# Linear attention into a tanh-shrink MLP: two loads swapped, the work of batch 1 and the phi of batch 2 spread over later slots, two matmuls moved ahead of a spread

## The chip, the cores and the metric

The kernel runs on one core of one Trainium2 chip. The metric is the device time of one execution in microseconds (us). Executions of one kernel agree within some 0.4%; the clock granted to TensorE was 0.997 to 1.0. Times inside an execution are us from the start of its span, as the profile gives them.

## The reference, cut to what matters

```python
q, k, v: (8, 8, 576, 64) float32; w_in: (512, 2048); w_out: (2048, 512)
phi(x) = where(x > 0, x, exp(x) - 1) + 1
kv  = einsum('bhsd,bhse->bhde', phi(k), v);   z = sum(phi(k), axis=2)
num = einsum('bhsd,bhde->bhse', phi(q), kv)
den = einsum('bhsd,bhd->bhs', phi(q), z)[..., None] + 1e-6
x   = (num / den), laid out as (4608 tokens, 512)
h   = x @ w_in;   out = (h - tanh(h)) @ w_out
```

## The kernel before

TensorE does nine chunks of 512 tokens. A chunk has a first matmul in 16 column blocks of 4 matmuls (h = x w_in), then a second one in 16 slots of 4 (g w_out). The attention of the next batch is slipped in between: `s1[fi]` holds what follows column block fi, `s2[s]` what follows slot s. Each engine runs its own list in program order. `xT` is x transposed, its four head pairs being p = 0 to 3.

From chunk 1 on the first matmul goes round six PSUM banks; a pair of blocks is freed when VectorE has written `gT` from it:

```python
dense = Banks([0, 1, 2, 3, 4, 5])       # block 10 of chunk 1 comes to bank 4 again, block 4's
attn = Banks([6, 7])                    # kv, denominators and numerators of the next batch
def l1act2(fi, h, gT):                  # after each odd block
    th = mpool.tile([128, 2, 512], F32, name="th")
    nc.scalar.activation(th, h, AF.Tanh)
    nc.vector.tensor_sub(gT[:, fi:fi + 2, :], h, th)
```

phi is an exp on ScalarE and two operations on VectorE, called the rest below:

```python
e = exp(x)                  # ScalarE
r = max(x, 0) + 1           # VectorE
y = min(e, r)               # VectorE
```

For batch 1 and most of batch 0 a spread (a group of small matmuls with `sel`) copies each head's reciprocal denominators to the partitions where they are needed. From batch 2 on the reciprocal denominators go through memory: four small writes to `ds`, then two broadcasting reads into `rdb`, all on SyncE's queue; the numerators are scaled with `rdb`.

```python
def a_spread(b):
    ...
    for t in range(4):
        nc.sync.dma_start(out=ds[:, t, :], in_=rden_t[b][32 * t:32 * t + H, :])
    ...
    for hh in range(2):
        nc.sync.dma_start(out=rdb[64 * hh:...], in_=ds[4 * hh:...].partition_broadcast(64))

def a_num(b, p):            # two banks, so numerator 3 waits until numerator 1 is scaled
    ps = num_mm(b, p, attn)
    nc.vector.tensor_mul(xT[:, p, ...], ps, rdb[:, p, ...])
```

The loads of batch c + 2 (k, q, v) are issued at the start of chunk c by GpSimd, behind a gate that reads the last column of the transposed q of batch c + 1, so they wait for that transposing DMA, which is on SyncE's queue as well, in order with the output stores:

```python
s1[0].append(lambda: (gate(qT_t[n1]), load_k(n2), load_q(n2), load_v(n2)))
```

## Time and profile before

| | us |
|---|---|
| time, median of 3 runs at first | 293.31 (293.09 to 293.58) |
| span of the profiled run | 291.8 |
| TensorE busy | 285.5 |
| VectorE, ScalarE busy | 175.1, 139.7 |
| second matmul of chunk 0 starts | 31.07 |
| first and second matmul of chunk 1 start | 50.24, 65.93 |
| third numerator of chunk 1; chunk 2 starts | 79.31; 80.72 |

TensorE's ends are modelled, so idle time is not read from the busy sum but from starts: a start, plus the number of matmuls times 0.216, against the next group's start. The prediction shows the lines.

### The profile page before, as it was taken

The numbers are of one execution on the slowest core, as the hardware profiler recorded it, in microseconds if no ns is written. First come the engines' busy times: TensorE is split into PE (matmuls) and PEld (weight loads), VectorE is DVE, ScalarE is ACT, GpSimd is POOL, SyncE is SP. The second block draws the span as 40 slices with busy tenths as digits, with TensorE's granted clock in tenths as the row PEclk, the third lists the DMA queues.
The fourth block names the chain that finished last, engine by engine and source line by source line (L and its number), as shares of the span: only waits on it lengthen the run. The fifth ranks groups of instructions, "written<-read, shape, count | busy, mean of one in ns | idle before, by whom it ended". The sixth has DMA issues, their size and how long they took to land.

```text
span 291.8 us, 4505 instructions
## 1 busy us (share of the span) xinstructions
PE 285.5 (98%) x1803; PEld 134.5 (46%) x1803; DVE 175.1 (60%) x266; ACT 139.7 (48%) x168; POOL 33.7 (12%) x56
## 2 busy tenths in 40 slices
PE   8999999999999999999999999999999999999994
PEld 3544464454454444444454444444544444444443
DVE  4759958987468674776478637865581457106600
ACT  4938548846354733465345534751551155126411
POOL 8674030110030003000300030000000000000000
PEclk9999999999999999999999999999999999999999
DMA  7999999997999768965895579666117310130032
GB/s 105 193 202 212 208 206 215 194 183 149 249 158 161 175 128 137 197 146 121 136 223 123 123 139 197 146 138 139 30 38 165 73 36 0 43 83 19 0 74 72
DMA packets 39093, 38.94 MB, mean 133 GB/s; under 512 B 16352, under 2 KB 33824, under 8 KB 38304
## 3 DMA queue, kind: packets, MB, share of 16 engines
q0 software_dynamic: 17568, 18.35, 39.0%
q1 hardware_dynamic: 21344, 20.17, 30.9%
q8 instruction: 14, 0.23, 0.3%
q10 hardware_dynamic: 160, 0.13, 0.1%
q14 instruction: 7, 0.06, 0.1%
HBM read 43.91 MB, written 9.55 MB: 183 GB/s over the span
## 4 chain that ended last, share of the span: by engine, by line
PE 85%; DMA 11%; POOL 2%; issue 1%; DVE 0%; POOLq 0%
PE ps_all L387 39%; PE ps_all L366 38%; DMA v<-in_v_dram 6%; DMA w_in_sb<-in_moe_w_in_dram 3%; PE ps_all L199 2%; DMA kraw<-in_k_dram 2%; PE ps_all L317 2%; PE ps_all L618 1%; PE ps_all L276 1%; POOL v L419 1%; PE ps_all L177 1%; POOL qraw L90 0%; PE ps_all L320 0%; POOL qraw L93 0%; POOL w_out_sb L115 0%
## 5 line engine op out<-in xcount | busy, mean ns | idle before, releaser
L366 PE MATMUL ps_all<-xT,w_in_sb 128*128 128x512 bf16 x574 | 127.6, 379 | 0.0
L387 PE MATMUL ps_all<-w_out_sb,gT 128*128 128x512 bf16 x560 | 127.5, 379 | 0.0
L373 DVE TENSOR_TENSOR gT<-ps_all,th 128x1024 bf16<-128x1024 f32 x64 | 77.9, 1218 | 59.2 <-ACT th L372 59.2
L372 ACT ACTIVATE th<-ps_all 128x1024 f32<-128x1024 f32 x64 | 65.6, 1025 | 57.1 <-PE ps_all L366 46.5
L366 PEld LDWEIGHTS <-w_in_sb 128*128 128x128 bf16 x574 | 55.0, 98 | 66.1 <-issue 0.3
L387 PEld LDWEIGHTS <-gT 128*128 128x128 bf16 x560 | 54.2, 98 | 64.2
L396 ACT COPY osb<-ps_all 128x512 f32<-128x512 f32 (+1 forms) x36 | 20.9, 583 | 71.8 <-PE ps_all L387 52.6
L328 DVE TENSOR_TENSOR xT<-ps_all,rdb 128x512 bf16<-128x512 f32 x24 | 16.5, 691 | 13.7 <-PE ps_all L317 11.2
L134 ACT ACTIVATE e<-qraw 128x1152 bf16<-128x1152 bf16 x16 | 18.5, 1160 | 8.2 <-DMA qraw<-in_q_dram 8.2
L134 ACT ACTIVATE e<-kraw 128x1152 bf16<-128x1152 bf16 x15 | 17.5, 1164 | 0.3 <-DMA kraw<-in_k_dram 0.3
L136 DVE TENSOR_TENSOR qp<-e,r 128x1152 bf16<-128x1152 bf16 x16 | 12.1, 758 | 8.0 <-ACT e L134 7.2
L136 DVE TENSOR_TENSOR kp<-e,r 128x1152 bf16<-128x1152 bf16 x15 | 11.4, 759 | 7.9 <-ACT e L134 6.9
L383 POOL COPY g<-qT 1x1 bf16<-1x1 bf16 x5 | 0.9, 178 | 119.2 <-DMA qT<-qp 119.2
L378 DVE TENSOR_TENSOR gT<-ps_all,th 128x512 bf16<-128x512 f32 x16 | 10.3, 686 | 2.4 <-ACT th L377 1.7
L377 ACT ACTIVATE th<-ps_all 128x512 f32<-128x512 f32 x16 | 9.2, 598 | 4.4 <-PE ps_all L366 3.2
L447 PE MATMUL ps_all<-zero 128*128 128x512 bf16 x29 | 9.2, 480 | 1.2 <-DVE zero L405 1.2
L317 PE MATMUL ps_all<-qT,kz 128*128 128x512 bf16 x28 | 10.1, 379 | 0.0
L135 DVE TENSOR_SCALAR r<-qraw 128x1152 bf16<-128x1152 bf16 x16 | 7.3, 454 | 2.1 <-DMA qraw<-in_q_dram 2.1
L199 PEld LDWEIGHTS <-kp 64*128 64x128 bf16 x216 | 6.4, 94 | 2.5 <-issue 2.1
L285 DVE RECIPROCAL rden<-den 128x144 f32<-128x144 f32 x7 | 7.4, 1053 | 0.2
L199 PE MATMUL ps_all<-vp,kp 64*128 64x136 bf16 x216 | 7.4, 220 | 0.0
L394 DVE COPY osb<-ps_all 128x128 f32<-128x128 f32 x1 | 0.3, 292 | 11.6 <-PE ps_all L618 11.6
(85 smaller groups left out, 123.6 us busy)
## 6 DMA issues: line engine op xcount, KB each, us to landing
out_dram<-osb SPq DMA_DIRECT2D x70, 128.0 KB
rdb<-ds SPq DMA_DIRECT2D x12, 576.0 KB
kraw<-in_k_dram POOLq DMA_DIRECT2D x7, 576.0 KB, 7.1
qraw<-in_q_dram POOLq DMA_DIRECT2D x7, 576.0 KB, 9.1
v<-in_v_dram POOLq DMA_DIRECT2D x7, 576.0 KB, 11.6
w_in_sb<-in_moe_w_in_dram POOLq DMA_DIRECT2D x6, 256.0 KB, 8.7
w_out_sb<-in_moe_w_out_dram POOLq DMA_DIRECT2D x3, 512.0 KB, 14.7
qraw<-in_q_dram POOLq DMA_DIRECT2D x2, 288.0 KB, 4.4
```

What stands on the lines that cost most here:

```text
L134: return (lambda: nc.scalar.activation(e, x, AF.Exp), lambda: nc.vector.tensor_scalar(r, x, 0.0, 1.0, ALU.max, ALU.add), lambda: nc.vector ...
L136: lambda: nc.vector.tensor_tensor(y, e, r, ALU.min))
L199: nc.tensor.matmul(ps[hg][:, i, :], kp[r, i, j].rearrange("p h d -> p (h d)"), vp[r, i, j, :], start=(j == 0), stop=(j == J - 1))
L317: nc.tensor.matmul(ps, kz[:, p // 2, p % 2, 0:128], qT[:, p % 2, 0:8, p // 2, :], start=True, stop=True)
L328: nc.vector.tensor_mul(xT[:, p, S * b:S * b + 512].rearrange("p (j t c) -> p j t c", j=8, t=4), ps.rearrange("p j (t c) -> p j t c", t=4), ...
L366: nc.tensor.matmul(h, w_in_sb[:, 2 * (p % 2) + p // 2, fi * 128:(fi + 1) * 128], xT[:, p, c * 512:(c + 1) * 512], start=(n == 0), stop=(n ...
L372: nc.scalar.activation(th, h, AF.Tanh)
L373: nc.vector.tensor_sub(gT[:, fi:fi + 2, :], h, th)
L377: nc.scalar.activation(th, h, AF.Tanh)
L378: nc.vector.tensor_sub(gT[:, fi, :], h, th)
L387: nc.tensor.matmul(o, gT[:, fi, i * 128:(i + 1) * 128], w_out_sb[:, fi, :], start=(fi == 0), stop=(fi == NF - 1))
L396: nc.scalar.copy(osb[:, f0:f1], o[:, f0:f1])
```

## The change

Its intent, as far as the code shows it: kv of batch 1 no longer waits for v (half a quarter of w_out, wanted first, is loaded first, and kv goes from slot 7 to slot 9); the rests of phi make room for xT on VectorE; and the opening does two matmuls ahead of a spread. With these come two moves: kv and the denominators of batch 2 (`a_den`, `a_spread`) come two column blocks later in chunk 1, and the transposing DMA of its q (`a_qT_dma(2)`) goes from slot 13 to slot 15 of chunk 0.

```diff
-    load_v(1)
     for n in range(2):
+        if n == 1:
+            load_v(1)
         nc.gpsimd.dma_start(out=w_out_sb[:, 8 + 2 * n:10 + 2 * n, :], ...)
 ...
-            s2[7].append(lambda: (a_qT_pe(1, 0, side), a_kv(1, side), a_qT_pe(1, 1, side)))
-            s2[8].append(lambda: b0_scale_rest(side))
-            s2[9].append(lambda: (a_den(1, side), num1(), a_split(1)))
-            s2[11].append(lambda: spread1(0))
+            s2[7].append(lambda: a_qT_pe(1, 0, side))
+            s2[8].append(lambda: a_qT_pe(1, 1, side))
+            s2[9].append(lambda: a_kv(1, side))
+            s2[10].append(lambda: (b0_scale_rest(side), a_den(1, side), num1(), a_split(1)))
+            s2[12].append(lambda: spread1(0))
 ...
-            s2[11].append(lambda: (exp2(qs, q_t, qp_t, "qp", 0), rest2(qs[0])))
+            s2[11].append(lambda: exp2(qs, q_t, qp_t, "qp", 0))
             s2[12].append(lambda: exp2(qs, q_t, qp_t, "qp", 1))
-            s2[13].append(lambda: (spread1(1), exp2(ks, k_t, kp_t, "kp", 0), rest2(qs[1]), a_qT_dma(2)))
-            s2[14].append(lambda: rest2(ks[0]))
+            s2[14].append(lambda: (spread1(1), exp2(ks, k_t, kp_t, "kp", 0), rest2(qs[0])))
+            s2[15].append(lambda: (rest2(qs[1]), a_qT_dma(2)))
 ...
-            s1[8 if c == 1 else 5].append(lambda: a_kv_cols(n1, attn))
-            s1[10 if c == 1 else 8].append(lambda: (a_den(n1, attn), a_spread(n1)))
+            s1[10 if c == 1 else 5].append(lambda: a_kv_cols(n1, attn))
+            s1[12 if c == 1 else 8].append(lambda: (a_den(n1, attn), a_spread(n1)))
 ...
-            s1[1].append(lambda: a_kphi(2, 1))
-            s1[3].append(lambda: (a_vp(2, 0), a_vp(2, 1)))
+            s1[1].append(lambda: (exp2(ks, k_t, kp_t, "kp", 1), rest2(ks[0])))
+            s1[3].append(lambda: rest2(ks[1]))
+            s1[5].append(lambda: (a_vp(2, 0), a_vp(2, 1)))
 ...
-            order = [((0, 0), (0, 1)), ((2, 0), (2, 1), (0, 2), (0, 3), (2, 2), (2, 3)),
+            order = [((0, 0), (0, 1)), ((2, 0), (2, 1)), ((0, 2), (0, 3), (2, 2), (2, 3)),
 ...
-                if n == 1:
+                if n == 2:
                     open2()          # the second spread
 ...
-            if c == 2 and fi == 1:   # blocks 0 and 1: pairs 0, 1 of both, then pairs 2, 3
+            if c in (1, 2) and fi == 1:
 ...
-            elif c != 2 or fi > 1:
+            elif c not in (1, 2) or fi > 1:
```

## The prediction

> **What bounds the kernel now.** First the page. TensorE is busy for 98% of the span at full clock, so I look for the few tenths in which it waits.
>
> ```profile
> PE 285.5 (98%) x1803; PEld 134.5 (46%) x1803; DVE 175.1 (60%) x266; ACT 139.7 (48%) x168; POOL 33.7 (12%) x56
> ...
> PEclk9999999999999999999999999999999999999999
> ```
>
> Then TensorE's own timeline (start, length, engine, line, instructions). Sixty-two 512-column matmuls begin at 17.68 and the next group at 31.07: 13.39/62 = 0.216 us each. With that cadence I find every hole. The first transposes of batch 1 take nine times 0.058, to 38.50; kv starts at 38.87. A step from full-size matmuls to a smaller tile costs 0.10 wherever it occurs (80.72 + 24 x 0.216 = 85.90, kv at 86.00), so 0.27 of that hole is the wait for v. The second spread, 17.02, waits about 0.4. At 46.20 there is 0.1 over the step.
>
> ```profile
> 17.02 0.73 PE L240 MATMUL ps_all<-rden,sel 32*128 32x128 f32 x16 [0.22 <-DVE xT L244]
> 17.68 13.55 PE L366 MATMUL ps_all<-xT,w_in_sb 128*128 128x512 bf16 x62
> 31.07 7.07 PE L387 MATMUL ps_all<-w_out_sb,gT 128*128 128x512 bf16 x32
> 37.98 0.67 PE L164 MATMUL ps_all<-ident,qp 128*128 128x128 bf16 x9
> 38.87 1.66 PE L177 MATMUL ps_all<-v,kp 64*128 64x192 bf16 x36 [0.22 <-DMA v<-in_v_dram]
> ...
> 50.24 8.07 PE L366 MATMUL ps_all<-xT,w_in_sb 128*128 128x512 bf16 x36
> ```
>
> Chunk 1's first matmuls, from 50.24, need 36 x 0.216 = 7.77 and take 7.91 up to the 0.10 step before kv at 58.24: 0.14 of waiting. So all that can be gained is about 0.4 + 0.27 + 0.1 + 0.14 = 0.9 us.
>
> Third, the timelines of VectorE and ScalarE around the start of chunk 1, because three parts of the change move work there. The reader should see how full they are.
>
> ```profile
> 51.77 0.45 DVE L135 TENSOR_SCALAR r<-kraw 128x1152 bf16<-128x1152 bf16 x1
> 52.33 0.76 DVE L136 TENSOR_TENSOR kp<-e,r 128x1152 bf16<-128x1152 bf16 x1
> 53.50 1.23 DVE L373 TENSOR_TENSOR gT<-ps_all,th 128x1024 bf16<-128x1024 f32 x1 [0.41 <-ACT th L372]
> 54.64 0.45 DVE L135 TENSOR_SCALAR r<-kraw 128x1152 bf16<-128x1152 bf16 x1
> 55.19 0.76 DVE L136 TENSOR_TENSOR kp<-e,r 128x1152 bf16<-128x1152 bf16 x1
> 55.87 1.22 DVE L373 TENSOR_TENSOR gT<-ps_all,th 128x1024 bf16<-128x1024 f32 x1
> 57.00 0.82 DVE L189 COPY vp<-v 128x1152 bf16<-128x1152 bf16 x2
> 57.74 2.35 DVE L373 TENSOR_TENSOR gT<-ps_all,th 128x1024 bf16<-128x1024 f32 x2
> ```
>
> Back to back, a gT pair costs VectorE 1.13, a phi rest (r and kp) 1.23, the vp pair 0.74. ScalarE is tied to the landing of q of batch 2: exp at 47.34, four evacuations and two more exps, tanh at 52.41.
>
> Fourth, the end of chunk 1. The scaling there waits for rdb, the broadcast reciprocal, which lands at about 77.8.
>
> ```profile
> 77.87 1.48 DVE L328 TENSOR_TENSOR xT<-ps_all,rdb 128x512 bf16<-128x512 f32 x2 [2.39 <-DMA rdb<-ds]
> ```
>
> Its chain: den at 61.24, rden ready 64.06, the small ds writes issued at 64.09 but done only at 69.4, rdb issued at 69.44, landing 8.4 later. The DMA share falls from 1.19 to 0.69 at 68 to 69 us: the small writes finish just after the loads of batch 3.
>
> **What the Trainium skill says.** "PSUM — Partial Sum Buffer", section "PSUM bank collisions raise a hardware error", tells one to guard PSUM by bank and quadrant, not by address. The trace agrees: the second spread writes other columns than VectorE is reading, yet starts at 17.02, just after the reader ended at 16.97. "TensorE: Matmul & The Clock Gate", section "Architectural detail: the array is 16× 32×32, not 1× 128×128", says that ScalarE and VectorE are strict FIFO; here the rests and gT pairs do run in program order, so a late one delays all behind it. "DMA: Bandwidth & Descriptors", section "Issuing engines are not separate DMA queues", says that transfers of all issuers share 16 engines and interleave; the ds writes that take 5.3 us under the loads and 2.3 (92.72 to 95.00) at their end agree.
>
> **The change part by part.**
>
> *w_out before v.* Landings before, from issue plus time to landing: q 35.9, v 38.8, first half quarter 40.05, second 41.35, last quarter 43.85. The queue moves 256 KB in about 1.25 us, so the half quarter now lands near 37.2 and v near 40.05; everything behind is where it was, q of batch 2 at 47.2 included. Slot 8 needs w_out near 38.6 and kv in slot 9 needs v near 41: neither waits. Gain 0.27.
>
> *Opening.* The two matmuls need the same xT as the spread waited for, so they start at 17.02 too. The spread then pays its 0.10 step in the open, and xT of the third pair arrives 0.05 too late. Loss about 0.15.
>
> *Slots 7 to 15.* The same work, walked with the measured pieces from 38.13 (37.98 and the opening's 0.15): transposes 0.52, slot 8 0.86, transposes 0.52, slot 9 0.86, step and kv 0.10 + 1.59, slot 10 0.86, the rest of batch 0 0.11, step and den 0.10 + 0.36, which is 44.01. VectorE's kz is ready 1.0 after kv (43.6), in time for den at 43.65. Numerators 0.11 + 0.86, slots 11 and 12 1.73: 46.71. The split's result followed den's first matmul by 3.2 before (42.91 to 46.14), so the first spread starts at 46.94 with 0.13 of wait, about what it had. Spread 0.23, two slots 1.73, step and spread 0.33, slot 15 0.86: chunk 1 begins at 50.1 instead of 50.24. On ScalarE exp of k moves behind the third evacuation, which removes the 0.14 wait for bank 2; the fourth ends at 52.50 (47.34 + three exps of 1.07 + four copies of 0.46, with small rounding), still ahead of bank 3's use at 52.72. The chain from q's landing has the same members, so tanh of the first pair is again at 52.4 and its gT at 53.48. The interleaving of matmuls covers the later xT (pair 3 ready 50.83, wanted 51.2).
>
> *Phi of k in chunk 1.* This is where I expect the loss. Both rests of k now lie between the gT pairs: gT01 53.48, rest 54.62, gT23 55.85, rest 56.98, gT45 58.21, done 59.43. Before, 0.74 of vp lay between gT23 and gT45; now 1.23. TensorE meanwhile comes sooner to bank 4, which gT45 frees for column block 10, because kv and its step (1.27) moved from behind block 8 to behind block 10: 50.1 + 0.04 + 10 x 0.864 = 58.8 plus 0.08 of wait on gT23 = 58.85. It waits until 59.48: 0.63. Then six blocks (5.18), kv (1.27), den (0.46): the second matmul begins at 66.39, before 65.93. The loss is 0.46 net, and all the gains above are inside it: earlier arrival only lengthens this wait, since gT45 hangs on q's landing.
>
> *Den later.* Den is two blocks later: 63.44 against 61.24; rden 66.25 against 64.06. Also the transposing DMA of q goes from slot 13 to 15, behind four output stores on the sync queue (each 0.6): near 54.1 instead of 51.93. It gates the loads of batch 3, so they move by 2.2 as well. ds again ends just behind them, near 71.6, and rdb lands near 80.0 instead of 77.8. TensorE has two banks for the numerators; the third one, at 79.31 before and 79.77 now, needs the first scaled: 80.0 + 0.69 + 0.05 = 80.74. Wait 0.97. Before, the same sum was 78.61, 0.70 of slack. Since den and loads both have to slip for this, I count 0.75 of it. Chunk 2's interleaving was there before and covers pairs 2 and 3. Later chunks are as before: rden of batch 3 to its use is 13 us.
>
> Sum: 0.46 + 0.75 = 1.2; 293.31 + 1.2 = 294.5.
>
> **The rivals.**
> 1. *The holes close and nothing opens.* Then 0.27 + 0.14 is saved and 0.15 lost: 293.0; with the opening at its best, 292.6. For it: the landing times, and that the moves look meant to give VectorE room. Against it: the VectorE sum of five pieces, 1.14 + 1.23 + 1.13 + 1.23 + 1.22 = 5.95, which starts at 53.48.
> 2. *Only the bank wait.* rdb comes in time because ds escapes the loads: 293.31 + 0.46 = 293.8. For it: without loads ds takes 2.3, not 5.3. Against it: the loads' gate slips as far as den.
> 3. *rdb in full*: 0.46 + 0.97 = 1.4, or more if the output stores of chunk 1 slow it: 294.8 to 295.3.
> 4. *w_out late for slot 8.* It has 1.4 us of room by the landing times; unlikely.
>
> **Range and chances.** The middle is 294.5. The low end, 293.2, takes rival 1 nearly whole; the high end, 295.4, is rival 3 with slower stores. Two per cent is 5.9 us; the holes that can close sum to 0.9 and the losses I can find to 1.5. Faster 0.01, same 0.98, slower 0.01.
>
> **What would show it.** Right: TensorE's wait for v is gone and kv of batch 1 starts near 41; in chunk 1 it idles some 0.6 us before column block 10 (near 59), released by a gT of VectorE; the second matmul of chunk 1 begins 0.3 to 0.6 later than 65.93; the scaling at the end of chunk 1 waits for rdb until about 80, and the third numerator waits for it. From chunk 2 on the two kernels keep a constant distance. Wrong: block 10 starts without a hole (then VectorE was quicker or began earlier than 53.48), or rdb lands by 79.0, which leaves the numerators free; a loss before 50 us would mean that an arrival in slots 8 to 10 was misjudged.

## The result, and the profile after

The changed kernel took 294.48 us (median of 5 runs, 294.2 to 295.33), the kernel before 293.38 (5 runs, 293.09 to 293.61). The ratio is 1.0042, with a 95% interval of 1.0024 to 1.0059: slower by 0.4%, within the 2% band. A ratio here is the mean time of one kernel's fast runs over that of the other's of the same rounds, so it is not quite the ratio of the medians.

The spans of the two profiled runs are 291.8 and 292.6. The execution profiled before (293.57) was the second slowest of its five and the one profiled after (294.36) the second fastest, so the traces differ by less than the medians. Where the 0.8 comes in is read from the starts on TensorE's two timelines:

| start of | before | after | after - before |
|---|---|---|---|
| second matmul of chunk 0 | 31.07 | 31.18 | +0.11 |
| first matmul of chunk 1 | 50.24 | 50.06 | -0.18 |
| second matmul of chunk 1 | 65.93 | 65.89 | -0.04 |
| first numerator of chunk 1 | 77.16 | 77.12 | -0.04 |
| third numerator of chunk 1 | 79.31 | 80.16 | +0.85 |
| first matmul of chunk 2 | 80.72 | 81.57 | +0.85 |
| last tile of the output | 284.30 | 285.14 | +0.84 |

TensorE's timeline after (start, length, engine, line, operation):

```profile
16.97 0.59 PE L366 MATMUL ps_all<-xT,w_in_sb 128*128 128x512 bf16 x2 [0.22 <-DVE xT L244]
17.50 0.73 PE L240 MATMUL ps_all<-rden,sel 32*128 32x128 f32 x16
18.16 13.19 PE L366 MATMUL ps_all<-xT,w_in_sb 128*128 128x512 bf16 x60
31.18 7.07 PE L387 MATMUL ps_all<-w_out_sb,gT 128*128 128x512 bf16 x32
...
40.92 1.66 PE L177 MATMUL ps_all<-v,kp 64*128 64x192 bf16 x36
...
50.06 9.93 PE L366 MATMUL ps_all<-xT,w_in_sb 128*128 128x512 bf16 x44
59.93 1.24 PE L199 MATMUL ps_all<-vp,kp 64*128 64x136 bf16 x36
...
78.41 1.03 PE L387 MATMUL ps_all<-w_out_sb,gT 128*128 128x512 bf16 x4
80.16 0.38 PE L317 MATMUL ps_all<-qT,kz 128*128 128x512 bf16 x1 [0.72 <-DVE xT L328]
```

The opening: from the first line's start to 31.18 it is 14.21, where 17.02 to 31.07 was 14.05: 0.16 lost, since the pair waits as the spread had waited and the step to the small tile now shows. kv at 40.92: slot 9 is over at 39.96 + 0.86 = 40.82, and the 0.10 of the step follows, so nothing is left of the wait for v. Chunk 1: 44 matmuls are 9.50 of work, but from 50.06 to the step before kv at 59.93 it is 9.77: a hole of 0.27. In the kernel before the 36 matmuls ahead of kv waited 0.14, and chunk 1 began 0.18 later; so the second matmul of chunk 1 starts 0.04 earlier than it did. The last two lines: the slot ends at 78.41 + 0.86 = 79.27 and the third numerator starts at 80.16, a hole of 0.89; the profile prints less, as it counts from the modelled end.

The chain of work that ended last shows the first hole (start, length, what):

```profile
57.70 1.23 DVE gT L373
58.93 0.04 issue
58.97 1.02 PE ps_all L366 x4
```

Block 10 of chunk 1 (58.97) is released by VectorE's third gT. VectorE's timeline shows how it got there:

```profile
52.43 0.76 DVE L136 TENSOR_TENSOR qp<-e,r 128x1152 bf16<-128x1152 bf16 x1
53.11 1.22 DVE L373 TENSOR_TENSOR gT<-ps_all,th 128x1024 bf16<-128x1024 f32 x1
54.24 0.45 DVE L135 TENSOR_SCALAR r<-kraw 128x1152 bf16<-128x1152 bf16 x1
54.73 0.76 DVE L136 TENSOR_TENSOR kp<-e,r 128x1152 bf16<-128x1152 bf16 x1
55.40 1.22 DVE L373 TENSOR_TENSOR gT<-ps_all,th 128x1024 bf16<-128x1024 f32 x1
56.54 0.45 DVE L135 TENSOR_SCALAR r<-kraw 128x1152 bf16<-128x1152 bf16 x1
57.02 0.76 DVE L136 TENSOR_TENSOR kp<-e,r 128x1152 bf16<-128x1152 bf16 x1
57.70 1.22 DVE L373 TENSOR_TENSOR gT<-ps_all,th 128x1024 bf16<-128x1024 f32 x1
```

gT, rest, gT, rest, gT without a gap. The first gT comes right behind the rest of q (52.43), not behind a wait for tanh: VectorE itself was the bound, but barely. Tanh began at 51.99; before, gT followed tanh's start by 1.09 (52.41, 53.50), which would give 53.08 here.

The second hole is released by the scaling, which waits for the broadcast. VectorE's line after, against 77.87 before:

```profile
79.42 1.89 DVE L328 TENSOR_TENSOR xT<-ps_all,rdb 128x512 bf16<-128x512 f32 x3 [3.98 <-DMA rdb<-ds]
```

And SyncE's queue, where the broadcast is issued, before:

```profile
51.93 3.23 SPq L153 DMA_TRANSPOSE qT<-qp  x1
...
64.09 1.28 SPq L305 DMA_DIRECT2D ds<-rden  x4
69.44 1.12 SPq L308 DMA_DIRECT2D rdb<-ds  x2
```

and after:

```profile
53.50 2.92 SPq L153 DMA_TRANSPOSE qT<-qp  x1
65.78 1.29 SPq L305 DMA_DIRECT2D ds<-rden  x4
70.77 1.12 SPq L308 DMA_DIRECT2D rdb<-ds  x2
```

The small writes are issued 1.7 later, and what the broadcast waits for, their end, comes 1.3 later. The transposing DMA, on which the loads of batch 3 hang, starts 1.6 later.

### The profile page after: what moved, and what is told of

The parts are those of the page before. It is cut to its first block, busy times and chain, and to the rows that moved or that the text cites. A ratio compares the mean times of both kernels' runs of the same rounds, so it can differ in the third digit from the quotient of the medians.

```text
span 292.6 us, 4508 instructions
## 1 busy us (share of the span) xinstructions
PE 286.1 (98%) x1803; PEld 134.7 (46%) x1803; DVE 174.9 (60%) x266; ACT 139.4 (48%) x168; POOL 33.9 (12%) x56
## 4 chain that ended last, share of the span: by engine, by line
PE 82%; DMA 9%; DVE 4%; POOL 1%; issue 1%; SPq 1%; ACT 1%; DVEq 0%; POOLq 0%
PE ps_all L366 39%; PE ps_all L387 34%; DMA rdb<-ds 3%; DMA out_dram<-osb 2%; DMA v<-in_v_dram 2%; PE ps_all L199 2%; PE ps_all L317 2%; DMA ds<-rden 1%; DVE gT L373 1%; PE ps_all L276 1%; ACT osb L396 1%; PE ps_all L177 1%; DVE r L135 1%; DVE qp L136 1%; POOL kraw L90 0%
```

## The experiments

The theory after the result: the loss is the late broadcast ahead of the third numerator; the bank wait ahead of block 10 eats up what was gained earlier. Rivals: the bank wait or the opening is the loss; or the loss comes from the slots of chunk 0. Experiments named `b_...` start from the kernel before, the others from the changed one unless said otherwise. All had 5 rounds. In the first call the kernel before took 293.32 (9 runs), in the second 293.35, in the third 293.42, in the last 293.29.

### The changed kernel again, as control (`after_again`)

> The changed kernel itself, as the control of this call. Theory (late broadcast): 0.8 to 1.4 us slower than before; the hole in TensorE ahead of the third numerator of chunk 1 is again 0.7 to 1.0 us, and the one ahead of column block 10 of chunk 1 lies between 0.2 and 0.7, larger the later q of batch 2 lands. Rival (the loss is noise of two placements): within 0.3 us of before.

294.97 us; ratio to before 1.0054 (1.0041 to 1.0068). In its trace the third numerator starts at 80.24, where the slot ended at 79.25: a hole of 0.99; the hole ahead of block 10 is 0.26. Its median lies 1.65 above before, while the trace's holes and gains make some 0.9. The traced execution was the second fastest of five in the first result and the fastest here (spans of 292.6 both times, the others up to 293.7), so other executions lose more.

One thing varies that the change does not touch: in the traces of all versions the opening's wait for xT ends between 16.74 (`b_den_late`) and 17.88 (`b_open`), here at 16.96.

### Nothing waits for the broadcast (`rdb_unread`, wrong result)

```diff
-                rdb[:, p, :, 0:8, :].rearrange("p t j c -> p j t c"))
+                (fake if b == 2 else rdb[:, p, :, 0:8, :]).rearrange("p t j c -> p j t c"))
```

(`fake` is a constant tile; the last 64 tokens likewise.)

> The changed kernel with one edit, a wrong result on purpose: the numerators of batch 2 are scaled by a constant tile, so nothing waits for the broadcast reciprocal, which is still made, sent and broadcast. Theory (late broadcast): the 0.9 us hole ahead of the third numerator is gone, the time is 0.8 to 1.0 us below the changed kernel's, level with before to within 0.3. Rival (the bank wait ahead of column block 10, or the opening, is what costs): the hole goes but the time falls by under 0.3, since the loss was already there.

293.91 us, 1.06 below the control; ratio to before 1.0019 (1.0006 to 1.0032). TensorE's timeline:

```profile
59.59 1.02 PE L367 MATMUL ps_all<-xT,w_in_sb 128*128 128x512 bf16 x4 [0.41 <-DVE gT L374]
...
79.03 1.03 PE L388 MATMUL ps_all<-w_out_sb,gT 128*128 128x512 bf16 x4
79.89 0.38 PE L318 MATMUL ps_all<-qT,kz 128*128 128x512 bf16 x1
```

79.03 + 0.86 = 79.89: the hole ahead of the third numerator is gone, and the time it was worth came back: 1.06 of the control's 1.65. The broadcast is the main loss. But here the expectation missed: the kernel is not level with before to within 0.3; 0.6 is left. The first line above shows why in this execution: chunk 1 began at 50.23, block 10 was due at 50.23 + 40 x 0.216 = 58.87 and began at 59.59, so the bank wait was 0.72. In this trace exp of q waited for its load and ran at 47.56, against 46.46 in the trace of the changed kernel above, and VectorE's first gT waited for tanh (ScalarE and VectorE):

```profile
47.56 1.16 ACT L135 ACTIVATE e<-qraw 128x1152 bf16<-128x1152 bf16 x1 [0.77 <-DMA qraw<-in_q_dram]
...
53.72 1.23 DVE L374 TENSOR_TENSOR gT<-ps_all,th 128x1024 bf16<-128x1024 f32 x1 [0.36 <-ACT th L373]
```

### The rest of k's second half behind the third gT (`k_late`), alone and with the unread broadcast

```diff
-            s1[3].append(lambda: rest2(ks[1]))
-            s1[5].append(lambda: (a_vp(2, 0), a_vp(2, 1)))
+            s1[5].append(lambda: (rest2(ks[1]), a_vp(2, 0), a_vp(2, 1)))
```

> The changed kernel with the rest of k's second half moved behind the third gT pair, so that the bank of column block 10 comes free 1.2 us earlier. Theory: the hole ahead of block 10 vanishes and the second matmul of chunk 1 starts 0.2 to 0.3 earlier (near 65.6), but the broadcast lands no earlier because it hangs on the loads, so the third numerator waits longer by the same amount, and the time stays within 0.2 us of the changed kernel's. Rival (the bank wait is the loss): the time falls by 0.3 to 0.6.

294.59 us; ratio 1.0043 (1.0029 to 1.0056), so 0.38 below the control's median, with intervals that overlap. Its trace shows the expected exchange. Chunk 1's 44 matmuls run from 50.34 to 59.84 (kv at 59.94, less the step): 9.50, no hole. Chunk 1 itself began 0.30 later than in the control's trace, so the second matmul started at 65.91 and not near 65.6. The hole ahead of the third numerator grew:

```profile
78.42 1.03 PE L387 MATMUL ps_all<-w_out_sb,gT 128*128 128x512 bf16 x4
80.41 0.38 PE L317 MATMUL ps_all<-qT,kz 128*128 128x512 bf16 x1 [0.96 <-DVE xT L328]
```

78.42 + 0.86 = 79.28 to 80.41 is 1.13. The small writes were issued at 65.79 (control 65.76), the broadcast at 71.23 (70.97): what was gained at block 10 was lost again in this trace. Whether the 0.38 of the medians is real is not settled.

> Both edits at once, a wrong result on purpose. Theory: with the broadcast out of the way the bank wait counts as well, so 0.2 to 0.3 us (up to 0.5 where q lands late) below the run with the unread broadcast alone, and 0.1 to 0.4 below before. Rival (the two waits are independent and simply add): the same here, but then moving k alone would have shown it too.

293.31 us; ratio 1.0007 (0.9993 to 1.0020): with both waits out of the way the changed kernel is not told apart from before (293.32). It did not get 0.1 to 0.4 below before, as expected. The bank wait's own share is not settled by the times: the median is 0.60 below that of the unread broadcast alone, the mean only 0.36, and the five runs here are spread over 1.1 (293.02 to 294.11), so the intervals of the two versions overlap. That the bank wait costs something is read from the traces: 0.27 in the first, 0.72 in that of `rdb_unread`, none in this one (44 matmuls from 50.90 to 60.39). The execution traced here was one of the two slow ones (294.08). In it the opening's wait for xT ended at 17.81, 0.84 later than in the changed kernel's first trace, and the delay was still there at 66.46, where the second matmul of chunk 1 starts.

### The two delays of the broadcast, one at a time (`b_den_late`, `b_qT_late`, `b_both_late`)

```diff
 # b_den_late
-            s1[10 if c == 1 else 8].append(lambda: (a_den(n1, attn), a_spread(n1)))
+            s1[12 if c == 1 else 8].append(lambda: (a_den(n1, attn), a_spread(n1)))
 # b_qT_late
-            s2[13].append(lambda: (spread1(1), ..., rest2(qs[1]), a_qT_dma(2)))
+            s2[13].append(lambda: (spread1(1), ..., rest2(qs[1])))
+            s2[15].append(lambda: a_qT_dma(2))
 # b_both_late: both
```

> The kernel before with only the denominators of batch 2 (and the spread after them) moved two column blocks later in chunk 1, as the change has it; the loads of batch 3 stay where they were. Theory (the small writes finish just behind those loads, whenever they were issued): they are issued near 66.0 instead of 64.1 but still end near 69.4, the broadcast lands near 78, the third numerator does not wait, and the time is within 0.2 us of before. Rival (the small writes take 5.3 us from their issue): the broadcast is issued near 71.2 and lands near 79.6, the third numerator waits about 1.0, 0.9 to 1.1 us slower.

293.54 us, ratio 1.0012 (0.9998 to 1.0025): no loss that the interval can tell from none.

> The kernel before with only the transposing DMA of q of batch 2 moved two slots later, behind the last output stores of chunk 0; the denominators stay where they were. The transpose starts near 54.4 instead of 51.9 and the loads of batch 3 slip by about 2 us. Theory (the writes finish just behind the loads): although issued at 64.1 they end near 71.3, the broadcast lands near 79.6, the third numerator waits 0.6 to 1.0, and the time is 0.6 to 1.0 us above before. Rival (they take 5.3 us from their issue, or the prediction's 'both have to slip'): no wait, within 0.2 us of before.

293.22 us, ratio 0.9998 (0.9986 to 1.0011): no loss. Here my theory missed: I had expected the small writes to end behind the loads however early they were issued.

> The kernel before with both of these moves and nothing else of the change. Theory: as with the transpose alone, the broadcast lands near 79.6 and the third numerator waits 0.6 to 1.0; 0.6 to 1.0 us slower than before. If the two delays add, the broadcast lands after 80.5 and it is 1.5 us slower or more. If neither matters (the cost of the change is elsewhere), within 0.2 us of before.

294.56 us, ratio 1.0041 (1.0029 to 1.0054): the loss of the change, 1.2 us, from these two moves alone. It is more than the 0.6 to 1.0 expected and less than the 1.5 named for delays that add. In its trace the third numerator starts at 80.49, where its slot ended at 78.35 + 0.86 = 79.21: a hole of 1.28.

```profile
78.35 1.03 PE L387 MATMUL ps_all<-w_out_sb,gT 128*128 128x512 bf16 x4
80.49 0.38 PE L317 MATMUL ps_all<-qT,kz 128*128 128x512 bf16 x1 [1.12 <-DVE xT L328]
```

SyncE's queue in `b_den_late`:

```profile
65.55 1.28 SPq L305 DMA_DIRECT2D ds<-rden  x4
69.75 1.12 SPq L308 DMA_DIRECT2D rdb<-ds  x2
```

in `b_qT_late`:

```profile
63.80 1.29 SPq L305 DMA_DIRECT2D ds<-rden  x4
69.65 1.12 SPq L308 DMA_DIRECT2D rdb<-ds  x2
```

and in `b_both_late`:

```profile
65.72 1.28 SPq L305 DMA_DIRECT2D ds<-rden  x4
71.33 1.12 SPq L308 DMA_DIRECT2D rdb<-ds  x2
```

What counts is the difference of the two starts in each pair, held against the end of the loads. The loads of batch 3 were issued from 57.14 in the first, from 59.51 and 59.76 in the other two, and the DMA share drops in the microsecond after 68 in the first, after 70 in the other two:

| | ds issued | loads end about | rdb issued | ds took | hole ahead of numerator 3 |
|---|---|---|---|---|---|
| before | 64.09 | 68.7 | 69.44 | 5.35 | 0 |
| den late | 65.55 | 68.5 | 69.75 | 4.20 | 0 |
| transpose late | 63.80 | 70.5 | 69.65 | 5.85 | 0 |
| both late | 65.72 | 70.8 | 71.33 | 5.61 | 1.28 |
| changed kernel | 65.78 | 69.9 | 70.77 | 4.99 | 0.89 |

All five fit one reading: under the loads the small writes take some 5.4 to 5.9 us, but they are through about 1 us (0.7 to 1.3) after the loads end, whichever comes first. Each delay alone leaves the other way out; both together close it. That each alone is harmless and both together cost 1.2 us is shown by the three runs; the rule for the small writes is fitted to these traces after the fact, one execution each, and no run tests it.

### The opening alone (`b_open`) and the order of the two loads alone (`b_wfirst`)

The edits are those of the diff above.

> The kernel before with the change of the opening alone (two matmuls of the second pair ahead of the second spread). Theory: the pair waits for the same xT as the spread did, then the step to the small tile shows; from the first of these instructions to the second matmul of chunk 0 it takes 0.10 to 0.20 us longer (14.05 before), the wait for v of batch 1 shrinks by as much, and the time is within 0.2 us of before. Rival (the opening gains): that stretch is shorter by 0.1 or more.

293.70 us, ratio 1.0009 (0.9996 to 1.0021). From 17.88 to 32.09 in its trace is 14.21 against 14.05: 0.16 longer, as expected. The time is not told apart from before.

> The kernel before with the order of the two loads changed alone: half a quarter of w_out ahead of v of batch 1, kv still in slot 7. Theory: v lands 1.2 us later, near 39.9, and the hole ahead of kv grows from 0.27 to 1.3 to 1.6; part of it is taken back before chunk 1's end because VectorE and ScalarE hang on q of batch 2 there, so 0.6 to 1.3 us slower than before. Rival (kv had slack, the order alone is free): within 0.2 us of before.

294.56 us, ratio 1.0040 (1.0027 to 1.0052). TensorE's line for kv:

```profile
40.44 1.66 PE L177 MATMUL ps_all<-v,kp 64*128 64x192 bf16 x36 [1.50 <-DMA v<-in_v_dram]
```

The order of the loads alone loses 1.1 us; it needs kv two slots later. In the changed kernel both are there and the wait is gone.

### Three attempts at a version that beats both (`k_late_qfirst`, `mix`, `mix3`)

`k_late_qfirst` is the changed kernel with k moved and, in chunk 1, the load of q of batch 3 ahead of the gate:

```diff
+            if c == 1:
+                s1[0].append(lambda: (load_q(n2), gate(qT_t[n1]), load_k(n2), load_v(n2)))
```

> The changed kernel with the rest of k's second half behind the third gT pair (as tried before) and, in chunk 1 only, the load of q of batch 3 issued ahead of the gate that waits for the transposing DMA, so that only k and v of batch 3 come behind it. By the last runs the small writes end at the earlier of 5.5 us after their issue and about 1 us after the loads. Theory: the loads then end near 68 instead of 70.7, the broadcast is issued near 69.3 and lands near 77.7, the third numerator does not wait; 0.8 to 1.2 us below the changed kernel, level with before to 0.3. Rival: q's load slows the transposing DMA by as much as it takes itself (near 3 us), the loads end where they did, and the time stays within 0.2 of the version with k moved alone.

294.66 us, ratio 1.0047 (1.0033 to 1.0061): the rival. The load ran beside the transposing DMA (SyncE's queue), so the loads did not end earlier and the rule above was not put to the test:

```profile
53.81 6.09 SPq L153 DMA_TRANSPOSE qT<-qp  x1
```

It is seen complete by the gate at 61.95, 8.1 after its start, where the changed kernel took 4.8 (53.50 to 58.27). k and v then start at 62.52, the loads end where they did (70.7), and the hole is still there (third numerator at 80.29).

`mix` starts from the kernel before, takes the loads, the slots 7 to 14 and the interleaving, but leaves the opening, kv and denominators of chunk 1 alone, and does the rests as early as it can:

```diff
+            s2[12].append(lambda: (exp2(qs, q_t, qp_t, "qp", 1), rest2(qs[0])))
+            s2[14].append(lambda: (spread1(1), exp2(ks, k_t, kp_t, "kp", 0), rest2(qs[1]), a_qT_dma(2)))
+            s2[15].append(lambda: rest2(ks[0]))
```

> A version meant to keep the gains and not the losses: the half quarter of w_out ahead of v, transposes and kv in slots 7 to 9, spreads in slots 12 and 14, the interleaved first two blocks of chunk 1; but the rests of phi go in as early as their inputs allow (first half of q in slot 12, second half with its transposing DMA in slot 14, first half of k in slot 15), and in chunk 1 kv and the denominators stay behind blocks 8 and 10 as before; the opening is that of before. Theory: no wait for v (0.27 less), no wait for bank 2 (0.14 less), perhaps 0.1 to 0.2 of new wait for the later xT, the broadcast in time; 0.0 to 0.4 us below before. Rival (the loss comes from the slots of chunk 0): 0.4 us or more above before.

293.65 us, ratio 1.0012 (0.9999 to 1.0024): not told apart from before, where a gain of up to 0.4 had been expected. The broadcast is in time, the wait for v is gone, but the 36 matmuls ahead of kv in chunk 1 take 50.13 to 58.22, 8.09 for 7.77 of work: pairs 2 and 3 of xT come late, behind the rest of q.

`mix3` takes pairs 0 and 1 of three blocks first, and puts the rest of k's second half behind the second gT.

> The mixed version once more, with its own new wait attended to: in its trace the first 36 matmuls of chunk 1 took 8.09 up to the step before kv where 7.77 is their work, since xT of the second pairs came late. Here three column blocks of chunk 1 do their first two pairs ahead of the second ones, and the second half of k's phi lies behind the second gT pair. Theory: those 0.3 us go, v and the broadcast stay in time, 0.2 to 0.5 us below before (293.0 or so). Rival (VectorE is full around the start of chunk 1, so the wait only moves to a bank or to kv): level with before to 0.2, with a hole of 0.2 or more at block 8, at kv or at block 10.

294.14 us, ratio 1.0027 (1.0013 to 1.0041): a miss, 0.85 above before. The rival had the place right, a new hole at kv, but said level with before. The 36 matmuls now take 7.77, but kv waits for vp, and the denominators follow later as well:

```profile
50.12 7.93 PE L366 MATMUL ps_all<-xT,w_in_sb 128*128 128x512 bf16 x36
58.31 1.32 PE L199 MATMUL ps_all<-vp,kp 64*128 64x136 bf16 x36 [0.26 <-DVE vp L189]
...
61.53 0.72 PE L276 MATMUL ps_all<-qT,kz 128*32 128x144 bf16 x16
```

In the kernel before, VectorE is busy for 9.27 of the 10 us from 50 to 60, and in the traces of `mix` and `mix3` each move of its work made another wait; `k_late` made none in chunk 1, but its broadcast was late. That no order could do better is not shown: `k_late` with the transposing DMA early again was not tried. No version here beat the kernel before.

## Why the prediction was right or wrong

The time was right, 294.5 against 294.48, and so was the mechanism: both waits opened where they were put. That the time fits to 0.02 is luck: two terms of the sum were off in opposite directions, and in the profiled pair they make 0.85 and not 1.2.

- *w_out before v.* Right. The half quarter landed at 36.8 (37.2 predicted), v at 39.6 (40.05); no wait in slots 8 to 10.
- *Opening.* Right: 0.16 for 0.15, in the changed kernel and alone.
- *Slots.* Right: chunk 1 began at 50.06 for 50.1. kv began at 40.92, where "near 41" was said.
- *Phi of k in chunk 1.* The hole is where it was put, block 10, released by a gT of VectorE. Its size is the term that was mis-sized for the profiled run: 0.63 predicted and 0.27 measured, so 0.46 net became -0.04 net at the second matmul (65.89, not 66.39). The step that failed is "the chain from q's landing has the same members, so tanh of the first pair is again at 52.4 and its gT at 53.48". In this execution the load of q was issued 0.43 earlier (38.38, not 38.81), and exp of q began 0.9 earlier (46.46, not 47.34) without a wait for it; the chain then hung on VectorE's own queue, which begins at the second spread, and gT came at 53.11. Of the 0.51 by which block 10 started earlier than predicted (58.97, not 59.48), 0.37 is this; the rest is that the five VectorE pieces and the handover took 5.86 instead of 6.00. TensorE was due there 0.15 earlier too, which gives back a part. With q late the term has its predicted size: 0.72 in the trace of `rdb_unread`. The landing of this load varies (in the traces where exp of q waited for it, exp began 8.0 to 8.7 after the load's issue), and the prediction treated it as fixed.
- *Den later.* Right in kind, and larger than counted: the hole is 0.89 (0.97 worked out, 0.75 counted). Rdb was predicted at 80.0 and came at 79.4, and the third numerator was due at 79.27 instead of 79.77; the two errors nearly cancel, so the size of this hole was in part luck too. "Both have to slip" proved exactly right by the three `b_` runs; "ds again ends just behind the loads" is only half of the rule, as the table above shows.
- *Sum.* In the profiled pair 0.85 instead of 1.2; in the medians 1.10, and 1.65 in the control's. That the executions without a profile lose more through a later q is argued from the trace of `rdb_unread`, not shown for them. A late opening is a rival for it that no run excludes: the trace of `k_late_rdb_unread`, 0.77 above that version's median, came out of the opening's wait for xT 0.84 later than the changed kernel's.
- *Rivals.* 1 is out (both holes opened), 2 is out (the broadcast was the larger one), 3 came nearest for the broadcast, 4 is out (no wait for w_out).

## What to carry to other kernels

Where the bounding engine is busy for 98% of the span, closing a hole of 0.3 us is worth something only if nothing downstream hangs on a clock of its own, such as a load's landing, another engine's full queue, or a broadcast through memory; look for these first, and work out each one's slack. When work is moved to a later place, list everything that is issued behind it on the same queue and everything gated by it: here a transposing DMA behind four stores delayed loads, and those, by the reading above, decided when four tiny writes came through. Two delays that are harmless alone can cost together what neither costs, so test them apart and together.

## What the Trainium skill lacked or had wrong

- "TensorE: Matmul & The Clock Gate", section "Back-to-back issue gap", gives about 131 ns for sustained 512-column matmuls and says that its formula's 216 ns counts too much there. These runs show 0.216 us each (13.39 us for 62, at full clock, with a weight load for each), so of its two figures the 216 ns is the one that fits.
- "DMA: Bandwidth & Descriptors", section "Queues, rings and completion order", says that the engines go round the queues packet by packet, but that section has no figure for what small transfers then suffer. Four writes of 4.5 KB on SyncE's queue took 4.2 to 5.9 us from issue to the next issue that waited for them where GpSimd's loads ran beside them, and 2.3 where the loads were ending (92.72 to 95.00).
- The same page, section "DMA Transpose (X-bar)", gives no figure for a transposing DMA with a load beside it: 4.8 us without one, 8.1 with one load of 576 KB beside it (start to the gate that saw it end; one execution each, other DMA traffic ran in both).
